# The last gV and the last gK of a decode-attention backward pass, each stored in two parts through two queues

## The chip, the cores and the metric

The kernel runs on one core of one Trainium2 chip. The metric is the device time of one execution in microseconds (us). Three runs of the kernel before took 887.74, 890.04 and 891.40 us; their median is 890.04 us. One more execution was taken with the profiler: it took 888.48 us, and its profile spans 886.3 us from the first to the last of the program's instructions.

## What is computed

One decoder block with pre-layernorm attention over a cache and a small ReLU network, for B = 2 sequences of one token, D = 640, H = 32 heads of width 128, a cache of Sk = 4096 positions, all in bf16. The output and the gradients of all inputs but one are wanted:

```python
def _A_ref(x, k_cache, v_cache, wq, wo):
    q = (x @ wq).reshape(B, Sq, Hq, Dh).transpose(0, 2, 1, 3)
    scores = einsum("bhqd,bhkd->bhqk", q, k_cache) * Dh ** -0.5
    p = softmax(scores)
    o = einsum("bhqk,bhkd->bhqd", p, v_cache)
    return o.transpose(0, 2, 1, 3).reshape(B, Sq, Hq * Dh) @ wo
h  = x + _A_ref(layernorm(x), k_cache, v_cache, wq, wo)
h2 = h + relu(layernorm(h) @ w1) @ w2
# outputs: h2, and the gradients to x, k_cache, v_cache, wq, wo, w1, w2 for a given grad_out
```

The two large results are the gradients to the caches: gK (`out_2`) and gV (`out_3`), each of 2 x 32 x 4096 x 128 bf16 numbers, which is 64 tiles of 1 MB (one for each pair of a sequence and a head). For one pair, gV is the outer product of the softmax weights with a row vector of 128, and gK the outer product of the scores' gradient with another such vector.

## The kernel before, in words

A tile of a cache or of its gradient is `[128 partitions, 32, 128]` bf16: partition p holds the 32 positions 32p to 32p+31, which are 8 KB that lie together in DRAM (`natural`, L440). So a store of one tile is 128 rows of 8 KB.

The work goes in two passes over the 64 pairs. The first (`p1_iter`, L452) loads K and V of a pair on SyncE's queue (L445), transposes K on TensorE, makes scores and softmax weights, and sums up what the later steps need of V. Between the passes, generators in the background (`middle_gen`, `fin_gen`, `gx_gen`) make the rest of the block and the gradients of the weights; `outer_tile` stores these from ScalarE's queue (L989). The second pass (`p2_iter`, L863) is at turn j, in this order:

- the last quarter of the scores' gradient of turn j-1 (`last_dp`, `score_grad`: the tile `gsp`, L858), and the rows `rb` for turn j (L882);
- two halves of gK of turn j-1 on VectorE (`outer_half`, L844), and its store from GpSimd's queue (L899);
- the V tile of turn j, loaded again as `Wt` or kept, transposed on TensorE in four groups (L424), copied out by ScalarE (L429), and multiplied with the gradient vector (L437);
- two halves of gV of turn j on VectorE (L844), in half of the pass with some rows on ScalarE (L930), and its store from GpSimd's queue (L931).

The first two turns store gV at L909, and the turns that run beside the first pass store gK at L941; neither concerns the last turn. The plan (L1160) ends with j = 63, whose gV is the last gV, and j = 64, which has only the last gK to make. A buffer goes back to its pool with `give`; the next writer of that buffer waits for the store's landing. After the last gK nothing takes a buffer, and the program ends when every queue's transfers have landed (SyncE waits for them at L1333).

GpSimd's queue carries only gV and gK stores in this part of the run, with a small copy (L884, `pp`) ahead of each turn. SyncE's queue carries loads, and two small stores of 10 rows of 256 B (`store_rows`, L675); the second of these is its last instruction before the end. At the start ScalarE's queue loads two inputs as 10 rows of 256 B (L208, L209).

Of the kernel before, what the change touches and what calls it, by code (L numbers as in the profile page):

```python
# [15 lines left out]
def kernel(  # L16
# [20 lines left out]
    nc = tc.nc  # L37
# [35 lines left out]
    def pst(shape, dtype, role, name):  # L73

        k = banks[role].pop(0)
        banks[role].append(k)
        return ps.tile(shape, dtype, tag=f"bank{k}", bufs=1, name=name)
# [11 lines left out]
    def take(tag, shape, name):  # L89
        assert free[tag] > 0, (tag, name)  # L90
        free[tag] -= 1
        k = homes[tag].pop(0)
        t = pools[k].tile(shape, BF16, tag=f"big{k}", bufs=1, name=name)
        home_of[id(t)] = (tag, k, t)
        return t

    def goes_to(tag):

        if owned[tag] > wanted.get(tag, len(pools)):
            for other in homes:  # L100
                if owned[other] < wanted.get(other, 0):
                    return other
        return tag

    def give(t, to=None):
        tag, k, _ = home_of.pop(id(t))
        to = to or goes_to(tag)
        owned[tag] -= 1
        owned[to] += 1
        free[to] += 1  # L110
        homes[to].append(k)
        given_at[k] = step[0]
# [282 lines left out]
    NP1 = len(pairs)  # L395
# [20 lines left out]
    def pair_transpose(nat, g, dve=False, busy=0):  # L416


        t_ps = pst([128, GT // 2, 128], FP32, "tps", "t_ps")
        warm(t_ps[:].rearrange("p j k -> p (j k)"), nat, g, busy)  # L420
        natf = nat[:].bitcast(FP32)
        for j in range(GT // 2):
            cc = (g * GT) // 2 + j
            nc.tensor.transpose(t_ps[:, j, :], natf[:, 2 * cc:2 * cc + 2, :].rearrange("p c k -> p (c k)"), ident_f[:])  # L424
        t_sb = mats.tile([128, GT // 2, 128], FP32, tag="XT", bufs=4, name="t_sb")
        if dve:
            nc.vector.tensor_copy(out=t_sb[:], in_=t_ps[:])  # L427
        else:
            nc.scalar.copy(out=t_sb[:], in_=t_ps[:])  # L429
        return t_sb  # L430

    def pair_matvec(dst, t_sb, g, vecs):
        v = t_sb[:].bitcast(BF16).rearrange("p j (k two) -> p j k two", two=2)
        for j in range(GT // 2):
            sc = g * GT + 2 * j
            for par in range(2):
                nc.tensor.matmul(dst[:, sc:sc + 2], lhsT=v[:, j, :, par], rhs=vecs[:, par, :],  # L437
                                 start=(par == 0), stop=(par == 1))

    def natural(cache, b, h):  # L440
        return cache[b, h].rearrange("(p sc) d -> p sc d", sc=NSC)
# [399 lines left out]
    def outer_half(dst, row, colp, k, short=0):  # L841
        n = HALF - short
        sl = slice(k * HALF, k * HALF + n)
        nc.vector.tensor_tensor(  # L844
            out=pairs_view(dst[:, sl, :]),
            in0=row.rearrange("p (a two) -> p a two", two=2)[:, None, :, :].to_broadcast([128, n, 64, 2]),
            in1=colp[:, sl, None, :].to_broadcast([128, n, 64, 2]), op=ALU.mult)

    def last_dp(j, c):

        b, h = turns[j]
        pair_matvec(c["dp"], c.pop("T3"), 3, gom[:, h, b, :, :])

    def score_grad(j, c):

        b, h = turns[j]
        gsp = small.tile([128, NSC, 2], BF16, tag="gsp", bufs=2, name="gsp")
        nc.vector.scalar_tensor_tensor(  # L858
            out=gsp[:], in0=c["dp"][:, :, None].to_broadcast([128, NSC, 2]), scalar=negdot[:, h, b:b + 1],
            in1=P_bf[:, b * H + h, :, None].to_broadcast([128, NSC, 2]), op0=ALU.add, op1=ALU.mult)  # L860
        return gsp

    def p2_iter(j, busy, act=0, own_gK=False, early=False):  # L863

        c = S2[j] if j < NP1 else None
        p = S2.get(j - 1)
        if p is not None:
            bp, hp = turns[j - 1]
            last_dp(j - 1, p)
            gsp = score_grad(j - 1, p)  # L870
        if c is not None:
            b, h = turns[j]
            go = gom[:, h, b, :, :]

            bank = pst([128, 512], FP32, "sps", "dp_ps")
            for k, col in enumerate((goc, qsc)):
                nc.tensor.matmul(bank[:, 128 + k * 128:256 + k * 128],  # L877
                                 lhsT=col[:, h, b:b + 1].to_broadcast([128, 128]), rhs=ident_bf[:],
                                 start=True, stop=True)
            c["dp"] = bank[:, 0:NSC]  # L880
            rb = mats.tile([128, 256], BF16, tag="rb", bufs=3, name="rb")
            nc.scalar.activation(out=rb[:], in_=bank[:, 128:384], func=ACT.Copy, scale=rt[:, b, h:h + 1])  # L882
            pp = small.tile([128, NSC, 2], BF16, tag="pp", bufs=2, name="pp")
            nc.gpsimd.tensor_copy(out=pp[:], in_=P_bf[:, b * H + h, :, None].to_broadcast([128, NSC, 2]))  # L884
            c.update(rb=rb, pp=pp)
            if act:
                pa = small.tile([128, 8], FP32, tag="pa", bufs=2, name="pa")
                nc.gpsimd.tensor_copy(out=pa[:], in_=P_bf[:, b * H + h, NSC - act:NSC])
            c["T0"] = pair_transpose(c["W"], 0, busy=busy)
        if p is not None:  # L890
            gK = take("g", [128, NSC, 128], "gK")
            outer_half(gK, p["rb"][:, 128:256], gsp, 0)
        yield
        if early:
            gV = take("g", [128, NSC, 128], "gV")
            outer_half(gV, c["rb"][:, 0:128], c["pp"], 0)
        if p is not None:
            outer_half(gK, p["rb"][:, 128:256], gsp, 1)
            nc.gpsimd.dma_start(out=natural(out_2, bp, hp), in_=gK[:])  # L899
            give(gK)  # L900
            del S2[j - 1]
        yield
        if c is None:
            return
        c["T1"] = pair_transpose(c["W"], 1, busy=busy)
        pair_matvec(c["dp"], c.pop("T0"), 0, go)
        if early:
            outer_half(gV, c["rb"][:, 0:128], c["pp"], 1)
            nc.gpsimd.dma_start(out=natural(out_3, b, h), in_=gV[:])  # L909
        yield  # L910
        c["T2"] = pair_transpose(c["W"], 2, busy=busy)
        pair_matvec(c["dp"], c.pop("T1"), 1, go)
        yield
        c["T3"] = pair_transpose(c["W"], 3, busy=busy)
        give(c["W"], "g" if j < H and j != 1 and owned["g"] < 3 else None)
        pair_matvec(c["dp"], c.pop("T2"), 2, go)
        if early:
            give(gV)
            yield
            last_dp(j, c)  # L920
            gsp = score_grad(j, c)
        else:
            gV = take("g", [128, NSC, 128], "gV")
            outer_half(gV, c["rb"][:, 0:128], c["pp"], 0)
            yield
            if own_gK:
                last_dp(j, c)
            outer_half(gV, c["rb"][:, 0:128], c["pp"], 1, act)
            for k in range(act):
                nc.scalar.activation(out=gV[:, NSC - act + k, :], in_=c["rb"][:, 0:128], func=ACT.Copy, scale=pa[:, k:k + 1])  # L930
            nc.gpsimd.dma_start(out=natural(out_3, b, h), in_=gV[:])  # L931
            give(gV)
            if own_gK:
                gsp = score_grad(j, c)
            yield
        if own_gK:
            gK = take("g", [128, NSC, 128], "gK")
            outer_half(gK, c["rb"][:, 128:256], gsp, 0)
            yield
            outer_half(gK, c["rb"][:, 128:256], gsp, 1)  # L940
            nc.gpsimd.dma_start(out=natural(out_2, b, h), in_=gK[:])  # L941
            give(gK)
            del S2[j]
            yield
# [275 lines left out]
    for n, (i, j) in enumerate(plan):  # L1220
# [18 lines left out]
        if j is not None:  # L1239
            while g2 is not None:  # L1240
                p2_step()
            if j < NP1:
                bg_until(("go", *turns[j]))
            g2 = p2_iter(j, 0, 8 if i is None and j <= H else 0, i is not None and plan[n + 1][1] is None, j < EARLY)
# [93 lines left out]
```

## Time and profile before

| | |
|---|---|
| median of 3 runs | 890.04 us (887.74 to 891.40) |
| profiled execution | 888.48 us |
| its span | 886.3 us |
| mean granted TensorE clock | 0.772 |
| busy: PE, DVE, ACT, POOL | 83%, 77%, 56%, 23% of the span |
| bytes moved | 361.85 MB, 408 GB/s over the span |
| last instruction of VectorE (second half of the last gK) ends | 869.40 us |
| last store issued (GpSimd, L899) | 869.70 us |
| span ends | 886.3 us |

The profile's page gives busy times of the engines, the span in 40 slices, the DMA queues with packets and bytes, and the issues with the time from issue to landing. Further views are taken from the trace: a timeline of instructions, waits (who waited for whom), and windows, which give for chosen stretches the busy time of each engine, the granted clock, the mean busy share of the core's 16 DMA engines ("DMA share": 0.06 is one engine of 16) and the rate in GB/s. The trace also keeps every DMA packet with its start, queue, duration and size, though not the number of the DMA engine that moved it. q0 is GpSimd's queue, q1 SyncE's, q10 ScalarE's.

### The profile page before, as it was taken

The page shows a single profiled execution, that of the slowest core. Times are in us where ns is not written, and L with a number is a line of the kernel's source. Part 1 is how long each engine was busy: PE and PEld are TensorE (multiplying, and loading weights), DVE is VectorE, ACT ScalarE, POOL GpSimd, SP SyncE. Part 2 cuts the span into 40 slices and gives each one's busy share as a digit, 9 for nine tenths or more (in the row PEclk, how much of TensorE's full clock was granted, in tenths as well). Part 3 has the DMA queues.
Part 4 walks back from the last instruction along what each step waited for, and adds up shares of the span by engine and source line. Part 5 has one row for each costly group of instructions (what it writes and reads, how often), then busy time and mean ns, then how long its engine had stood idle before and what let it go on. Part 6 is the DMA issues. An engine that isn't in the chain of part 4 may idle for free.

```text
span 886.3 us, 24732 instructions
## 1 busy us (share of the span) xinstructions
PE 738.8 (83%) x10143; PEld 618.2 (70%) x10143; DVE 681.3 (77%) x1281; ACT 498.8 (56%) x1292; POOL 204.1 (23%) x358
## 2 busy tenths in 40 slices
PE   4999899999999997988868767787877899867690
PEld 4887788888887886877757656665656667564550
DVE  2666787877788896876778887878788689989861
ACT  1444343446776664654536767777656766545570
POOL 1344433343312010000011332222222111111220
PEclk9999999999999999998995655555566755555555
DMA  9999999999879999999999999999999999999996
GB/s 380 423 420 414 417 409 417 425 423 412 332 295 402 423 423 426 422 426 425 414 398 396 418 421 421 420 413 420 419 416 403 417 425 420 425 425 425 425 424 275
DMA packets 56289, 361.85 MB, mean 408 GB/s; under 512 B 5680, under 2 KB 11760, under 8 KB 15472
## 3 DMA queue, kind: packets, MB, share of 16 engines
q1 hardware_dynamic: 34520, 211.13, 57.8%
q0 software_dynamic: 18432, 134.23, 36.5%
q10 hardware_dynamic: 3224, 14.92, 4.1%
q8 instruction: 80, 1.31, 0.5%
q14 instruction: 33, 0.27, 0.1%
HBM read 211.11 MB, written 149.13 MB: 406 GB/s over the span
## 4 chain that ended last, share of the span: by engine, by line
PE 35%; DMA 34%; DVE 16%; ACT 7%; issue 5%; SPq 0%; POOL 0%; ACTq 0%; POOLq 0%; DVEq 0%
DMA Vt<-in_A_v_cache_dram 15%; PE t_ps L424 14%; DMA out_dram<-gK 11%; PE m_ps L460 9%; DVE gK L844 4%; DVE gV L844 4%; DMA out_dram<-gV 3%; ACT gV L930 3%; PE s_ps L437 3%; DMA wqs<-in_A_wq_dram 3%; DVE pk L470 2%; PE u_ps L498 2%; ACT t_sb L429 2%; PE dp_ps L437 2%; DVE gxj L678 2%
## 5 line engine op out<-in xcount | busy, mean ns | idle before, releaser
L429 ACT COPY t_sb<-t_ps 128x512 f32<-128x512 f32 x479 | 273.1, 587 | 192.4 <-PE t_ps L424 188.6
L437 PEld LDWEIGHTS <-t_sb 128*128 128x128 bf16 x4096 | 178.9, 102 | 63.8 <-ACT t_sb L429 36.2
L424 PE MATMUL t_ps<-ident_f,Wt 128*128 128x128 f32 x832 | 198.6, 389 | 0.9 <-ACT t_sb L429 0.9
L470 DVE TENSOR_TENSOR pk<-Kt,ep 128x2048 bf16<-128x2048 bf16 (+1 forms) x128 | 152.6, 1193 | 47.1 <-ACT ep L524 29.0
L460 PE MATMUL m_ps<-pk,Vt 128*128 128x129 bf16 x2048 | 172.0, 223 | 19.9 <-DMA Vt<-in_A_v_cache_dram 18.8
L844 DVE TENSOR_TENSOR gK<-rb,gsp 128x2048 bf16<-128x2048 bf16 x128 | 153.4, 1227 | 13.3 <-DMA out_dram<-gV 8.5
L460 PEld LDWEIGHTS <-Vt 128*128 128x128 bf16 x2048 | 125.6, 99 | 50.2 <-issue 28.4
L424 PEld LDWEIGHTS t_ps<-ident_f,Wt 128*128 128x128 f32 x832 | 138.2, 202 | 31.9 <-issue 25.2
L424 PE MATMUL t_ps<-ident_f,Kt 128*128 128x128 f32 x1024 | 156.0, 286 | 2.5 <-DMA Kt<-in_A_k_cache_dram 1.9
L844 DVE TENSOR_TENSOR gV<-rb,pp 128x2048 bf16<-128x2048 bf16 (+1 forms) x128 | 142.7, 1139 | 16.3 <-DMA out_dram<-gK 9.9
L486 POOL COPY pk<-ep 128x16 bf16<-128x16 bf16 x80 | 83.6, 1046 | 158.4 <-ACT ep L524 80.0
L424 PEld LDWEIGHTS t_ps<-ident_f,Kt 128*128 128x128 f32 x1024 | 113.9, 145 | 5.0 <-ACT t_sb L429 2.7
L437 PE MATMUL dp_ps<-gom,t_sb 128*128 128x2 bf16 x2048 | 96.0, 168 | 25.1 <-ACT t_sb L429 24.7
L931 POOL DMA_DIRECT2D out_dram<-gV x62 | 33.0, 533 | 305.3 <-DVE gsp L858 135.1
L437 PE MATMUL s_ps<-qm,t_sb 128*128 128x2 bf16 x2048 | 87.4, 164 | 1.5 <-DVE t_sb L427 1.5
L986 ACT CAST ot<-o_ps 128x512 bf16<-128x512 f32 (+3 forms) x152 | 67.5, 491 | 8.4 <-DMA out_dram<-ot 5.2
L588 ACT CAST MT<-m_ps 128x128 bf16<-128x128 f32 x64 | 17.0, 266 | 94.5 <-PE m_ps L460 94.4
L899 POOL DMA_DIRECT2D out_dram<-gK x53 | 28.2, 533 | 135.4 <-DVE gK L844 104.9
L882 ACT ACTIVATE rb<-dp_ps,rt 128x256 bf16<-128x256 f32 x64 | 30.2, 472 | 44.7 <-PE dp_ps L877 43.4
L678 DVE CUSTOM_DVE_ANT_0 hbc<-wo_t,hbc 128x640 bf16<-128x640 bf16 x64 | 52.8, 825 | 0.3
L678 DVE CUSTOM_DVE_ANT_0 gxj<-wqs,gqr 128x1024 bf16<-128x1024 bf16 x40 | 48.7, 1217 | 1.0 <-DMA wqs<-in_A_wq_dram 0.8
L930 ACT ACTIVATE gV<-rb,pa 128x128 bf16<-128x128 bf16 x152 | 46.5, 392 | 3.9 <-DMA out_dram<-gK 3.9
(205 smaller groups left out, 758.2 us busy)
## 6 DMA issues: line engine op xcount, KB each, us to landing
Kt<-in_A_k_cache_dram SPq DMA_DIRECT2D x64, 1024.0 KB, 19.4
Vt<-in_A_v_cache_dram SPq DMA_DIRECT2D x64, 1024.0 KB, 15.5
out_dram<-gV POOLq DMA_DIRECT2D x64, 1024.0 KB, 14.9
out_dram<-gK POOLq DMA_DIRECT2D x64, 1024.0 KB, 15.0
Wt<-in_A_v_cache_dram SPq DMA_DIRECT2D x52, 1024.0 KB, 11.6
wq_t<-in_A_wq_dram SPq DMA_DIRECT2D x5, 1024.0 KB, 7.8
wo_t<-in_A_wo_dram SPq DMA_DIRECT2D x4, 1280.0 KB, 17.6
wqs<-in_A_wq_dram SPq DMA_DIRECT2D x5, 1024.0 KB, 22.3
```

The lines of the kernel that those rows point to most:

```text
L424: nc.tensor.transpose(t_ps[:, j, :], natf[:, 2 * cc:2 * cc + 2, :].rearrange("p c k -> p (c k)"), ident_f[:])
L429: nc.scalar.copy(out=t_sb[:], in_=t_ps[:])
L437: nc.tensor.matmul(dst[:, sc:sc + 2], lhsT=v[:, j, :, par], rhs=vecs[:, par, :], start=(par == 0), stop=(par == 1))
L460: nc.tensor.matmul(r["m"][:, 0:129], lhsT=r["V"][:, sc, :], rhs=r["pk"][sc // HALF][:, sc % HALF, 0:129], start=(sc == 0), stop=(sc == NSC ...
L470: nc.vector.tensor_tensor(out=p["pk"][k][:, 0:n, 0:128].rearrange("p s (a two) -> p s a two", two=2), in0=p["K"][:, sl, :].rearrange("p s ...
L486: nc.gpsimd.tensor_copy(out=col, in_=e)
L678: nc.vector.tensor_tensor_reduce(out=junk[0:kc, 0:width], in0=in0, in1=in1, scale=1.0, scalar=0.0, op0=ALU.mult, op1=ALU.add, accum_out=acc)
L844: nc.vector.tensor_tensor(out=pairs_view(dst[:, sl, :]), in0=row.rearrange("p (a two) -> p a two", two=2)[:, None, :, :].to_broadcast([128 ...
L882: nc.scalar.activation(out=rb[:], in_=bank[:, 128:384], func=ACT.Copy, scale=rt[:, b, h:h + 1])
L930: nc.scalar.activation(out=gV[:, NSC - act + k, :], in_=c["rb"][:, 0:128], func=ACT.Copy, scale=pa[:, k:k + 1])
L931: nc.gpsimd.dma_start(out=natural(out_3, b, h), in_=gV[:])
L986: nc.scalar.copy(out=ot[0:P, k, n0:n0 + nn], in_=o_ps[0:P, 0:nn])
```

## The change

The store of gK at L899 and the store of gV at L931 become calls of a helper. For all turns but the last it issues what was issued before. For the last gV (j = 63) and the last gK (j = 64) it issues partitions 0 to 119 from GpSimd's queue and partitions 120 to 127 from SyncE's queue.

```diff
+    def store(out_ap, t, last):
+
+        n = 120 if last else 128
+        nc.gpsimd.dma_start(out=out_ap[0:n], in_=t[0:n])
+        if last:
+            nc.sync.dma_start(out=out_ap[n:128], in_=t[n:128])
+        give(t)
@@ p2_iter
-            nc.gpsimd.dma_start(out=natural(out_2, bp, hp), in_=gK[:])
-            give(gK)
+            store(natural(out_2, bp, hp), gK, c is None)
@@ p2_iter
-            nc.gpsimd.dma_start(out=natural(out_3, b, h), in_=gV[:])
-            give(gV)
+            store(natural(out_3, b, h), gV, j == NP1 - 1)
```

The order of the instructions on TensorE, VectorE, ScalarE and GpSimd is the same in both kernels. SyncE has two more: after its last 10-row store, the 8 rows of the last gV and the 8 rows of the last gK.

## The prediction

> **What bounds the kernel now.** I read the slices first. The line "DMA" stands at 9 in nearly every slice, so transfers set the pace; only the last slice falls off, and the change touches nothing ahead of it.
>
> ```profile
> DMA  9999999999879999999999999999999999999996
> ...
> DMA packets 56289, 361.85 MB, mean 408 GB/s; under 512 B 5680, under 2 KB 11760, under 8 KB 15472
> ...
> q0 software_dynamic: 18432, 134.23, 36.5%
> ```
>
> Then the timeline of GpSimd's last issues. VectorE ends at 869.40; the last store is out 0.3 us later, and yet the span lasts to 886.3. So 16 us belong to transfers alone.
>
> ```profile
> 862.68 0.53 POOL L899 DMA_DIRECT2D out_dram<-gK  x1 [5.25 <-DVE gK L844]
> 864.96 0.53 POOL L931 DMA_DIRECT2D out_dram<-gV  x1 [1.74 <-DVE gV L844]
> 869.70 0.53 POOL L899 DMA_DIRECT2D out_dram<-gK  x1 [4.21 <-DVE gK L844]
> ```
>
> Then windows over those 16 us. The last two columns are the share of 16 DMA engines and the rate.
>
> ```profile
> 870.00:876.00 6.00, 0.00 (x0) 0.00 (x0) 0.00 (x0) 0.00 (x0) 0.23 (x1) 0.50 1.01 425
> 876.00:878.00 2.00, 0.00 (x0) 0.00 (x0) 0.00 (x0) 0.00 (x0) 0.00 (x0) 0.50 0.78 330
> 878.00:879.40 1.40, 0.00 (x0) 0.00 (x0) 0.00 (x0) 0.00 (x0) 0.00 (x0) 0.50 0.34 140
> 879.40:881.20 1.80, 0.00 (x0) 0.00 (x0) 0.00 (x0) 0.00 (x0) 0.00 (x0) 0.50 0.18 77
> 881.20:881.70 0.50, 0.00 (x0) 0.00 (x0) 0.00 (x0) 0.00 (x0) 0.00 (x0) 0.50 0.12 49
> 881.70:884.10 2.40, 0.00 (x0) 0.00 (x0) 0.00 (x0) 0.00 (x0) 0.00 (x0) 0.50 0.06 24
> 884.10:886.30 2.20, 0.00 (x0) 0.00 (x0) 0.00 (x0) 0.00 (x0) 0.00 (x0) 0.50 0.00 0
> ```
>
> The shares 0.18, 0.12 and 0.06 are three, two and one engine of 16: three still write after 879.4, two after 881.2, one from 881.7 to 884.1. That last stretch is 8 packets of 8 KB, one started every 0.306 us (2.45 us): one engine's sixteenth of a 128-row store. The waits of SyncE's queue say whose rows they are:
>
> ```profile
> SPq L1333 <- DMA out_dram<-gV: 42.6, 1, 42.6
> ...
> SPq L1333 <- DMA out_dram<-gK: 2.4, 1, 2.4
> ```
>
> The last gV has landed at 882.1 and the last gK 2.4 us later, so the late engine (I call it A) writes its 8 gV rows and then its 8 gK rows. By the packet list it ends at 884.13; the next ends at 881.68 (B), the others at 881.18, 879.45, and then 878.9 and earlier. **What is at stake is the tail of A**, not the 1 MB.
>
> **Which engine is A?** The packets carry no engine number, but an engine's packets follow each other with a fixed overlap of 3 ns, so its chain can be followed. Nearly all 8 KB packets in the last 40 us take 309 ns; those of 311 to 367 ns form one chain, which ends as A. So A is not merely last, it is slow: up to 876 its packets keep taking longer. In the second 10-row store of SyncE's queue one of the ten 256 B packets lies inside that chain (start from the span's start, queue, ns, bytes):
>
> ```
> 842.510 q0 312 8192
> 842.818 q1 18 256
> 842.832 q0 320 8192
> ```
>
> In the first one, at 781.6, one of the ten again runs straight into a lengthened packet. How many engines a small transfer uses follows from the page: 5680 packets under 512 B. The 350 other transfers (128 on q0, 203 on q1, 19 on q10) leave 16 completion packets of 4 B each, 5600; the 80 left are four 10-row transfers with 10 rows and 10 completions each. Ten rows use ten engines, and A was one of them both times.
>
> **The change, part by part.**
>
> 1. *GpSimd stores 120 rows.* Two issues of 0.53 us stay two issues. No row shows a 120-row store; an issue could lie between 0.50 us (120/128 of the row) and twice the row, 1.07 us. I take 0.53, its nearest row. It is covered either way: A's gK rows start at 881.7, 12 us after the issue, and the earliest engine's at about 873.3, 3 us after it. Without that cover it would cost at most 0.5 us.
> 2. *How the 120 rows fall on engines.* This is the open cost. Best for the change: fifteen engines take 8 rows each and A takes none; A then loses 16 packets and would end at 884.13 - 16 x 0.306 = 879.2, and B sets the end. Middle: A keeps its 8. Worst of the near cases: eight engines take 15 rows each, 14 more in the two stores, +4.3 us. The nearest rows are the 10-row ones, where the number of engines was a divisor of the rows: 120 = 15 x 8. Both 10-row transfers used A; if a transfer on fewer engines uses a fixed first set, fifteen include those ten, and A keeps its rows. I take 0, keeping -4.9 and +4.3 us on A.
> 3. *SyncE stores 8 rows, twice.* The issue row is 0.32 us (L675), on a queue idle from 839.5 on; nothing but the end stands behind it, so its new wait for VectorE holds up nobody. The 10-row store issued at 839.16 had its first packet at 842.7 and its last completion at 843.8. Issued near 865 and 870, the new rows should start near 868.5 and 873.3, take turns with the other queues' packets, and be gone by 875. They add one 8 KB packet to each of eight engines, twice. If A is among the eight (8 in 10, when the eight are part of the ten), A ends 2 x 0.306 = 0.61 us later; if not, nothing moves. I take +0.61, bounds 0 and +0.61.
> 4. *Two more completions at the end.* They land 8 us before A does; the end waits for A. Nothing.
>
> [...]
>
> **Sum.** 888.48 + 0 + 0.61 = 889.1 us for the profiled execution. The median of the runs is 1.56 us above that execution, so I forecast 890.04 + 0.61 = **890.6 us**. A measurement of this kernel can tell about 0.5% (4.45 us) from no change; this is within it.
>
> **Rivals.**
>
> *A is relieved.* The engine left out is A, in both stores (A would end at 879.2) or in the first alone (881.7). The end goes to B at 881.68, or 882.29 with the two SyncE rows on it: 884.13 less that is 1.84 to 2.45 us, so 887.6 to 888.2 us. For it: A is the slow engine and last; leaving out any fixed engine aims at something like it. Against it: A took part in both 10-row transfers. It can't give more than that, since B and the third are late too.
>
> *The 120 rows crowd onto fewer engines* (the slower side). If the store goes to eight engines, those have 15 rows instead of 8, 14 more over both stores: with A among them and the two SyncE rows, 4.28 + 0.61 = 4.9 us, 894.9 us, slower by 0.55%. It decides from the point where A itself has 9 rows or more in a store: each costs 0.306 us. If one engine took all 120, 37 us a store. Against it: ten rows used ten engines, not eight; for it: no store of an odd share of 128 on GpSimd's queue is in the trace.
>
> *The change does nothing that lasts.* The order of the other engines' instructions is the same, SyncE's two stores come after all else there, and if A is in neither set the end stays at 890.0 us. I count it with the forecast.
>
> **How the numbers follow.** Forecast (A keeps its rows, 0 to +0.61 us): 0.60. Relief: 0.25. Crowding: 0.10. Something not thought of: 0.05. The three runs before spread 3.7 us, so a median may move by half of that, 1.85 us. Range: from the relief's middle, 887.9, less about 1.1, to 890.6 plus 1.85: 886.8 to 892.5 us; it leaves out the crowding and the rest. Relief is -0.2% to -0.3%, so faster by over 0.5% needs scatter on top: 0.05. Slower by over 0.5% is most of the crowding: 0.09. Within: 0.86.
>
> **What would show it.** Windows over the tail: if A keeps its rows, the last stretch at 0.06 stays about 2.5 us long and ends some 0.6 us later after the last issue; the gap between the landings of gV and gK on SyncE stays 2.4 us. If A is relieved, that stretch shrinks below 0.6 us and the end comes within 12.6 us of the last issue instead of 14.4. If the rows crowd, a stretch near 0.50 (eight engines of 16) several us long appears. The packets on q0 tell the engines: a 120-row store's 8 KB packets number 240 in all, and the packets on q1 should be 16 rows and 16 completions more. The forecast is wrong if the slow engine isn't fixed from run to run, or if the odd shape makes GpSimd's issue much longer than 1 us.

## The result, and the profile after

The changed kernel takes 893.26 us (median of 13 runs, 891.81 to 897.09), the kernel before 888.81 us in the same rounds (13 runs, 887.53 to 891.68). The ratio of the runs is 1.0055, 95% interval 1.004 to 1.007: slower by 4.9 us (3.6 to 6.2), where the two medians differ by 4.45. In what follows, differences and their intervals are worked out from such ratios. The forecast was 890.6 us, and its range ended at 892.5. The profiled execution took 892.54 us, 4.06 more than that of before, with a span of 890.2 us.

The page of the changed kernel; its DMA line still stands at 8 or 9 up to the last slice, and the packets are those that the change must give:

```profile
span 890.2 us, 24736 instructions
...
DMA  9999999999889999999999999999999999999995
...
DMA packets 56321, 361.85 MB, mean 406 GB/s; under 512 B 5712, under 2 KB 11792, under 8 KB 15504
...
q1 hardware_dynamic: 34552, 211.26, 57.7%
q0 software_dynamic: 18432, 134.09, 36.4%
```

SyncE's queue q1 has 32 packets more (34,520 before): 16 rows and 16 completions. GpSimd's q0 has as many as before, though it lost 16 rows: so each 120-row store left 24 completions of 4 B instead of 16. That fits fifteen engines with 8 rows and one completion each, and a sixteenth without rows that posts 9 (8 and one); in the packet list, a run of ten 4 B packets of q0, 6 ns apart and without an 8 KB packet between them, stands at 871.92 to 871.97 us.

GpSimd's last issues in the timeline of the changed kernel (start, duration, line, what it stores, idle time before):

```profile
861.36 0.53 POOL L866 DMA_DIRECT2D out_dram<-gK  x1 [5.24 <-DVE gK L844]
863.63 0.54 POOL L866 DMA_DIRECT2D out_dram<-gV  x1 [1.74 <-DVE gV L844]
868.37 0.53 POOL L866 DMA_DIRECT2D out_dram<-gK  x1 [4.21 <-DVE gK L844]
```

and SyncE's:

```profile
839.56 0.32 SPq L675 DMA_DIRECT2D out_dram<-orow  x1
863.36 0.31 SPq L868 DMA_DIRECT2D out_dram<-gV  x1
868.11 0.28 SPq L868 DMA_DIRECT2D out_dram<-gK  x1
```

The last issue comes 1.33 us *earlier* than before (868.37 against 869.70), and the last row lands later: at 888.19, 19.8 us after that issue, where before it was 884.13, 14.4 us after. So in these two executions all of the loss lies in the transfers of the tail. Windows over it, after (the last two columns are the share of 16 DMA engines and GB/s):

```profile
868.00:872.00 4.00, 0.00 (x0) 0.00 (x0) 0.08 (x1) 0.00 (x0) 0.53 (x1) 0.50 1.01 411
872.00:876.00 4.00, 0.00 (x0) 0.00 (x0) 0.00 (x0) 0.00 (x0) 0.00 (x0) 0.50 0.97 352
876.00:880.00 4.00, 0.00 (x0) 0.00 (x0) 0.00 (x0) 0.00 (x0) 0.00 (x0) 0.50 0.78 282
880.00:884.00 4.00, 0.00 (x0) 0.00 (x0) 0.00 (x0) 0.00 (x0) 0.00 (x0) 0.50 0.25 90
884.00:888.20 4.20, 0.00 (x0) 0.00 (x0) 0.00 (x0) 0.00 (x0) 0.00 (x0) 0.50 0.06 25
```

and before, where one stretch of the same bounds stands beside the second of these:

```profile
872.00:876.00 4.00, 0.00 (x0) 0.00 (x0) 0.00 (x0) 0.00 (x0) 0.00 (x0) 0.50 1.02 426
```

Read the last two columns together. From 872 to 876 the engines are busy nearly all the time in both kernels, but move 352 GB/s instead of 426: 0.97/1.02 of the busy share, 0.83 of the bytes. **With packets of the same size, a full share with a lower rate means that each packet takes longer.** The last stretch, in which one engine writes alone (0.06), lasts 4.1 us (884.08 to 888.19) instead of 2.4.

The packet list says it row by row. Before, the last 256 packets of 8 KB on q0 take 309 ns each. After, the last 240 on q0 take 357 ns in the mean (some of them still belong to earlier stores), and the 16 rows of q1 up to 1329. In the 17 us up to the last landing, 53 of 343 packets of 8 KB on q0 are over 320 ns, and the list holds 15.0 us of engine time above 309 ns a packet, against 0.09 us before. The engine that ends last has this chain from 876.85 on, in ns (the list has no engine numbers, but an engine's packets follow each other, and a completion packet stands behind its share of each store):

```
931 640 593 533 329 309 526 607 609 659 644 | 8 x 309 (gV) | 8 x 309 (gK), ends 888.19
```

The 11 packets ahead of its own 16 rows belong to earlier, unsplit stores. They take 6.38 us where 11 x 309 ns would be 3.40: 2.98 us of the 4.06 by which the transfers end later. Followed further back, the chain most likely leads (at 871.92 two chains meet in the list) to one with a row of each of SyncE's stores, at 866.98 and 871.45, 309 ns each, and before that to lengthened packets of 314 to 369 ns (861.18 to 865.74), as the slow engine A has them. So the last engine is probably A again, and these two rows are another 0.61 us. SyncE's waits at the end show the last 8 rows once more:

```profile
SPq L1339 <- DMA out_dram<-gV: 17.7, 1, 17.7
...
SPq L1339 <- DMA out_dram<-gK: 2.4, 1, 2.4
```

gK lands 2.4 us after gV, as before: the last engine has 8 rows of gK, at the usual speed. It is late because it was held up *earlier*, while other engines moved rows of the split stores.

### The profile page after: what moved, and what is told of

Same layout as the page of the kernel before. It is cut to its first block, busy times and chain, and to the rows that moved or that the text cites. A ratio compares the mean times of both kernels' runs of the same rounds, so it can differ in the third digit from the quotient of the medians.

```text
span 890.2 us, 24736 instructions
## 1 busy us (share of the span) xinstructions
PE 740.7 (83%) x10143; PEld 620.8 (70%) x10143; DVE 681.2 (77%) x1281; ACT 498.9 (56%) x1292; POOL 203.4 (23%) x358
## 4 chain that ended last, share of the span: by engine, by line
PE 38%; DMA 29%; DVE 17%; ACT 7%; issue 5%; POOL 0%; ACTq 0%; SPq 0%; POOLq 0%; DVEq 0%
PE t_ps L424 16%; DMA Vt<-in_A_v_cache_dram 13%; DMA out_dram<-gK 9%; PE m_ps L460 9%; DVE gK L844 5%; DVE gV L844 4%; DMA out_dram<-gV 3%; PE s_ps L437 3%; ACT gV L937 3%; PE u_ps L498 3%; DVE pk L470 2%; DMA wqs<-in_A_wq_dram 2%; ACT t_sb L429 2%; DVE gxj L678 2%; PE dp_ps L437 2%
## 5 line engine op out<-in xcount | busy, mean ns | idle before, releaser
L460 PEld LDWEIGHTS <-Vt 128*128 128x128 bf16 x2048 | 125.8, 99 | 49.8 <-issue 29.0
```

The lines of the kernel that those rows point to most:

```text
L460: nc.tensor.matmul(r["m"][:, 0:129], lhsT=r["V"][:, sc, :], rhs=r["pk"][sc // HALF][:, sc % HALF, 0:129], start=(sc == 0), stop=(sc == NSC ...
```

## The experiments

Two theories. **First:** the number of rows of a store decides how its rows fall on the engines. With 128 rows, by this theory, the engines don't meet; with 120 they get in each other's way, and packets grow long. **Second:** SyncE's 8 rows do it, by a second queue that cuts into the engines' chains. In all edits `store` is the helper of the change, and the lines are shown against the changed kernel (the last edit against the kernel before); `...` stands for lines left out. Medians stand beside those of the kernel before on the same chip.

### One part alone: the 120 rows, or the 8

Only the 120 rows, with 8 rows of the last gV and gK not stored:

```diff
         nc.gpsimd.dma_start(out=out_ap[0:n], in_=t[0:n])
-        if last:
-            nc.sync.dma_start(out=out_ap[n:128], in_=t[n:128])
```

> Only the 120 rows are stored from GpSimd's queue; the 8 rows of the last gV and the last gK are left out of the output. Theory 1 (the 120-row store itself does the harm: its rows fall on the engines in another way than those of a 128-row store, so that engines get into each other's way): the packets on q0 are lengthened after 871 us as in the changed kernel (mean near 357 ns over the last two stores), and the time stays 3 to 5 us above before. Theory 2 (SyncE's 8-row stores do it: eight engines read eight neighbouring partitions at once): packets at 309 ns, time within 1 us of before.

Measured: 892.38 us (12 runs) against 889.17, ratio 1.0041 (1.0022 to 1.0061), +3.7 us. In the 17 us up to the last landing its 8 KB packets on q0 take 349 ns in the mean, 12.3 us of engine time above 309. Most of the loss is there without any row from SyncE.

The other part: 128 rows from GpSimd, and SyncE copies the last 8 partitions to a scratch tensor.

```diff
-        nc.gpsimd.dma_start(out=out_ap[0:n], in_=t[0:n])
...
+        nc.gpsimd.dma_start(out=out_ap, in_=t[:])
         if last:
-            nc.sync.dma_start(out=out_ap[n:128], in_=t[n:128])
+            sc = nc.dram_tensor(f"aside{len(asides)}", [8, NSC, 128], BF16).ap()
...
+            nc.sync.dma_start(out=sc, in_=t[120:128])
```

> GpSimd stores all 128 rows as before; SyncE also stores partitions 120 to 127 of the last gV and the last gK, to a place of their own in DRAM that is no output. Theory 1: 0 to 0.6 us above before (two more packets on some engines), only the 16 packets on q1 are long. Theory 2: 3 to 5 us above before, with long packets on q0 too.

Measured: 890.62 us (12) against 889.17, ratio 1.0014 (0.9994 to 1.0033), +1.2 us. GpSimd's packets take 316 ns, 2.95 us of engine time too much; SyncE's own rows still take up to 1732 ns. So the 8 rows run into others too, but there are few of them; at most 2.9 us by the interval, and not told from nothing.

### Is it the engine left without rows?

With a cut at 112 the same two queues are used, but the number of rows divides by the 16 engines: 16 x 7 rows.

```diff
-        n = 120 if last else 128
+        n = 112 if last else 128
```

> The cut at partition 112 in place of 120, so that both parts are multiples of 16 and every engine can have the same number of rows. If what harms is that one engine is left without rows: time as before, within 1 us. Theory 1 in the form that any store of other than 128 rows is dealt to the engines in neighbouring rows (7 each): long packets on q0, 2 to 5 us above before. Theory 2: 16 neighbouring partitions read at once, 3 us or more above before, longest packets on q1.

Measured: 892.01 us (12) against 889.17, ratio 1.0024 (1.0003 to 1.0045), +2.1 us. Each 112-row store leaves 16 completions, as a 128-row one does, so no engine sits out; yet the packets of q0 take 388 ns in the last 17 us, 21.6 us of engine time too much, more than in the changed kernel. So long packets need neither an idle engine nor its extra completions. (SyncE's 16 rows are in this run too; their packets take 3.7 us too much.) The time is less bad than the packets; probably less of the delay fell on the last engine, but that wasn't followed.

### The first theory made large

All 115 stores that go through the helper take 120 rows; 8 rows of each are not stored. SyncE stores nothing of them.

```diff
-        n = 120 if last else 128
+        n = 120
         nc.gpsimd.dma_start(out=out_ap[0:n], in_=t[0:n])
-        if last:
-            nc.sync.dma_start(out=out_ap[n:128], in_=t[n:128])
```

> All 115 stores of the helper (not only the last two) take 120 rows, and 8 rows of each are left out of the output: 7.5 MB less to move, 18 us at 424 GB/s. Theory 1: the last two stores of the changed kernel lost about 15 us of engine time on q0, 7.5 us each, 0.47 us of 16 engines; 115 of them cost 54 us, so 36 us above before (between 15 and 60, since loads in between may hide or add to it), with a mean of q0's 8 KB packets near 357 ns. Theory 2 and the theory that the tail alone matters: 10 to 18 us below before, packets near 310 ns.

Measured: 943.49 us (4) against 889.17, ratio 1.0598 (1.0558 to 1.0638): **54 us more, for 7.5 MB less to move.** Its windows in the second pass:

```profile
750.00:800.00 50.00, 35.45 (x295) 26.47 (x296) 38.97 (x58) 23.98 (x56) 6.77 (x14) 0.53 0.98 371
800.00:850.00 50.00, 28.41 (x242) 21.86 (x242) 38.29 (x52) 20.91 (x49) 5.83 (x12) 0.53 0.97 359
```

and of the kernel before:

```profile
750.00:800.00 50.00, 39.15 (x339) 29.05 (x338) 46.07 (x67) 27.67 (x64) 7.36 (x15) 0.53 1.01 425
800.00:850.00 50.00, 37.34 (x286) 24.87 (x285) 42.29 (x61) 28.30 (x58) 10.37 (x20) 0.53 1.01 424
```

It is the picture of the tail, held for hundreds of us: share nearly full, rate down by 13% and 15%. The page counts 6600 packets under 512 B, 5680 + 115 x 8: eight more completions a store, as reckoned above. All packets together took 877.9 us per engine before (mean of 16) and 909.6 here, 31.7 more. As the 920 rows left out would have taken 18.1 off, packets grew by 49.8 us per engine. The span is 56.9 us longer (943.2 against 886.3): 31.7 of it are packets, and for the other 25 an engine had, in the mean, no packet; what it waited for then was not followed. 8 KB packets of q0 went from 315 to 352 ns in the mean.

### Which side: the partitions or the place in DRAM

Twins: every one of the 115 stores stays whole, and GpSimd copies 8 more rows of the tile to scratch. They differ in the partitions alone that the 8 rows are read from: neighbours 0 to 7, or 0, 4, 8 to 28.

```diff
+        nc.gpsimd.dma_start(out=out_ap, in_=t[:])
...
+        nc.gpsimd.dma_start(out=sc, in_=t[0:8])
```

```diff
+        nc.gpsimd.dma_start(out=out_ap, in_=t[:])
...
+        nc.gpsimd.dma_start(out=sc, in_=t[0:32:4])
```

> Each of the helper's 115 stores keeps its 128 rows on GpSimd's queue and is followed there by 8 rows more, partitions 0 to 7, to a place of their own in DRAM: 7.5 MB more, 18 us at 424 GB/s. If engines that read neighbouring partitions at the same time hold each other up (theory 1 in the form of a shared way out of the partitions): the 8 packets take near 1 us each, as the longest ones on q1 did in the changed kernel, 5.6 us of engine time a store, so 30 to 70 us above before, and clearly more than its twin. If the cause lies on the DRAM side or in the number of rows: the same time as its twin.

> The twin: the same 8 rows more after each of the 115 stores, to the same place, but read from partitions 0, 4, 8 to 28 in place of 0 to 7. Theory of the shared way out: 12 to 25 us above before (the bytes alone) and few long packets. Theory of the DRAM side or of the number of rows: the same as its twin.

Measured: neighbours 1005.21 us (4 runs), ratio 1.1292 (1.1257 to 1.1326), +116 us; apart 934.32 us (4), 1.0493 (1.0466 to 1.0521), +45 us; before 889.28. Rows, bytes and target are the same. Packet time per engine rises by 65.6 us with neighbours and 30.9 apart, of which the 920 rows themselves are 18.1 (at 315 ns): 47.5 against 12.8 us of lengthening. On GpSimd's queue 808 packets of 8 KB take over 500 ns with neighbours, 184 apart and 239 before; their means are 336, 314 and 315 ns. A window of each, neighbours first:

```profile
750.00:800.00 50.00, 34.11 (x281) 24.18 (x280) 22.26 (x25) 22.28 (x49) 10.05 (x21) 0.54 0.95 372
```

```profile
750.00:800.00 50.00, 35.77 (x311) 27.28 (x310) 43.62 (x64) 23.93 (x55) 14.14 (x27) 0.50 0.97 384
```

**In these copies the choice of partitions that are read decides** (47.5 us of lengthening per engine against 12.8), so here packets are held up on the side of the tile, not of DRAM. That is shown; what reads of neighbouring partitions wait for is not, nor which row of a 120-row store goes to which engine. That the 120-row stores lose their time in the same way fits it but is argued.

Both cost more than expected (30 to 70 us and 12 to 25 us). The packets cover 65.6 us of the 116 and 30.9 of the 45; the rest was not followed. One candidate is to be seen in GpSimd's waits of the kernel with rows apart (in total us, times, longest):

```profile
POOL out_dram L867 <- DMA out_dram<-gV: 99.9, 26, 6.9
POOL out_dram L867 <- DMA out_dram<-gK: 52.6, 19, 5.7
```

With two issues a tile, GpSimd is held at issues until earlier stores of its own have landed; the kernel before has no such wait, and the one with 120 rows throughout has a single one of 1.4 us. How much of the 45 us this is stays open: the kernel with 120 rows throughout has its 25 us without packets in spite of that single wait.

### Halves: 64 rows, or half of each row

By rows:

```diff
-        n = 120 if last else 128
-        nc.gpsimd.dma_start(out=out_ap[0:n], in_=t[0:n])
-        if last:
-            nc.sync.dma_start(out=out_ap[n:128], in_=t[n:128])
+        for n in (0, 64):
+            nc.gpsimd.dma_start(out=out_ap[n:n + 64], in_=t[n:n + 64])
```

By columns:

```diff
-        n = 120 if last else 128
-        nc.gpsimd.dma_start(out=out_ap[0:n], in_=t[0:n])
-        if last:
-            nc.sync.dma_start(out=out_ap[n:128], in_=t[n:128])
+        for n in (0, 16):
+            nc.gpsimd.dma_start(out=out_ap[:, n:n + 16, :], in_=t[:, n:n + 16, :])
```

> Each of the helper's 115 stores leaves in two parts of 64 rows from GpSimd's queue, partitions 0 to 63 and 64 to 127. Each engine then has 4 rows of each part and all 16 are used evenly. Theory 1 (rows of a store with other than 128 rows are dealt so that engines read the same few groups of partitions): 30 to 80 us above before, q0's 8 KB packets well above 315 ns on the mean. If only uneven numbers of rows do harm: within 5 us of before.

> The control to the halves by rows: each of the 115 stores leaves in two parts of 128 rows with half of each row (4 KB). As many transfers and bytes in each, but rows from all partitions. Theory 1: within 8 us of before, no packets lengthened. If twice as many stores on GpSimd's queue do harm by themselves: the same excess as with the halves by rows.

Measured: by rows 950.77 us (4), ratio 1.0692 (1.0662 to 1.0723), +62 us; by columns 899.73 us (4), 1.0131 (1.0107 to 1.0154), +11 us; before 888.86. Both have 230 issues of 512 KB, and all partitions are stored. A window of each, first by rows:

```profile
750.00:800.00 50.00, 27.39 (x250) 20.73 (x247) 34.55 (x46) 19.20 (x44) 11.81 (x24) 0.50 0.98 358
```

then by columns:

```profile
750.00:800.00 50.00, 40.19 (x308) 28.45 (x308) 49.69 (x71) 26.71 (x63) 13.88 (x27) 0.52 1.02 419
```

With 64 rows an issue the rate falls to 358 GB/s at 0.98, and 8 KB packets of q0 take 361 ns; with 128 rows of half the length it stays at 419, and a 4 KB packet takes 161 ns (159 when undisturbed). So it isn't the second issue or the smaller store that lengthens packets, but that a store reads half of the partitions; and 64 rows, a multiple of 16, do it as well as 120. The 11 us by columns were more than expected: packet time rises by 13.0 us per engine (with 14,720 more packets of rows), which covers them. GpSimd's waits at its issues are there too:

```profile
POOL out_dram L866 <- DMA out_dram<-gV: 51.5, 29, 4.3
POOL out_dram L866 <- DMA out_dram<-gK: 49.4, 26, 5.0
```

What they cost was not told apart. Taking the 11 us off leaves some 50 of the 62 us to the halving by rows.

### One of the two stores

Only the last gV split:

```diff
-            store(natural(out_2, bp, hp), gK, c is None)
+            store(natural(out_2, bp, hp), gK, False)
```

Only the last gK:

```diff
-            store(natural(out_3, b, h), gV, j == NP1 - 1)
+            store(natural(out_3, b, h), gV, False)
```

> Only the last gV leaves in two parts; the last gK leaves whole, as before. Theory 1: each split store costs about half of the change's 4 to 5 us, so 1.5 to 3 us above before, with long packets on q0 from about 871 us that stop before the end. If only what stands at the very end counts: nothing measurable, below 1 us.

> Only the last gK leaves in two parts; the last gV leaves whole, as before. The gV alone came out at 0.7 us above before (-0.8 to +2.1). If the two parts of the change add up, the gK alone carries the rest: 3 to 4.5 us above before. If it takes both 120-row stores at work beside each other: 0 to 1.5 us above before.

Measured: gV alone 889.80 us (12) against 889.28, ratio 1.0008 (0.9991 to 1.0024); gK alone 890.42 us (12) against 888.86, 1.0021 (1.0002 to 1.0041). In each, q0's packets are held up by about 10 us of engine time in the 17 us up to the last landing (9.9 and 11.0), yet the end moves by 0.7 and 1.9 us. So the delay in all and the delay of the *last* engine are different things. Both splits together cost 4.9 us (3.6 to 6.2), more than the sum of the two, 2.6; the intervals are too wide to call that more than an impression. The gV alone lies below the 1.5 to 3 us that the first theory named, the gK alone between its two expectations.

### The queues exchanged

120 rows from SyncE, 8 from GpSimd:

```diff
-        nc.gpsimd.dma_start(out=out_ap[0:n], in_=t[0:n])
+        (nc.sync if last else nc.gpsimd).dma_start(out=out_ap[0:n], in_=t[0:n])
         if last:
-            nc.sync.dma_start(out=out_ap[n:128], in_=t[n:128])
+            nc.gpsimd.dma_start(out=out_ap[n:128], in_=t[n:128])
```

> The 120 rows of the last gV and gK leave from SyncE's queue and the 8 rows from GpSimd's. If the dealing of rows is a matter of the number of rows and not of the queue: 3 to 5 us above before, long packets on q1. If it is GpSimd's queue alone that deals 120 rows badly: within 1.5 us of before.

Measured: 891.86 us (9) against 888.86, ratio 1.0027 (1.0015 to 1.004), +2.4 us, between the two expectations. The packets decide: 8 KB packets that start after 870 us take 394 ns in the mean on SyncE's queue and 408 on GpSimd's. It is no matter of GpSimd's queue. The page also gives the engines once more:

```profile
q1 hardware_dynamic: 34790, 213.09, 58.3%
```

270 packets more than before: 240 rows and 30 completions, so 15 engines for each 120-row store, with no completions from the sixteenth on this queue.

### Is the last engine slow because of GpSimd's queue?

The last six turns' stores, whole, from SyncE:

```diff
+        (nc.sync if last else nc.gpsimd).dma_start(out=out_ap, in_=t[:])
...
-            nc.gpsimd.dma_start(out=natural(out_2, bp, hp), in_=gK[:])
...
+            store(natural(out_2, bp, hp), gK, j > NP1 - 6)
...
-            nc.gpsimd.dma_start(out=natural(out_3, b, h), in_=gV[:])
...
+            store(natural(out_3, b, h), gV, j >= NP1 - 6)
```

> The gV and gK of the last six turns leave whole, 128 rows, from SyncE's queue in place of GpSimd's. If the late engine is slow because of GpSimd's queue: its packets become regular (309 ns) in the last 40 us and the tail in which one engine writes alone shortens from 2.4 us towards nothing, 1 to 4 us below before. If it is slow by itself: time as before within 1 us, the tail as long as before. By theory 1 no long packets either way, as all rows leave in stores of 128.

Measured: 888.50 us (12) against 889.28, ratio 0.9985 (0.997 to 1.0), -1.3 us: the best of all, though not told from the kernel before. Whole stores from SyncE have hardly any long packets: 311 ns in the mean over the last 17 us, where those of the 120-row stores from SyncE took 394. Its tail:

```profile
880.00:882.00 2.00, 0.00 (x0) 0.00 (x0) 0.00 (x0) 0.00 (x0) 0.00 (x0) 0.50 0.43 180
882.00:884.00 2.00, 0.00 (x0) 0.00 (x0) 0.00 (x0) 0.00 (x0) 0.00 (x0) 0.50 0.16 66
```

A few engines still end late (0.16 is two to three of 16), but the last one writes alone for 0.7 us (883.71 to 884.41) instead of 2.4, and the last row lands 11.0 us after the last issue instead of 14.4. That is what was named for a slowness that comes from GpSimd's queue; the gain in time was not as clear. One chain of packets takes 313 to 361 ns up to 859.7 us, but GpSimd's own last packet stands at 860.6; after that, lengthened packets spread over several chains. So whether the engine is slow because of GpSimd's queue stays open.

## Why the prediction was wrong

**What bounds the kernel: right.** The tail of transfers sets the end, and the last engine's chain in it; the loss lies there. One reading was wrong: the packets of A do not keep taking longer up to 876. In the list of before, the last 8 KB packets over 309 ns stand at 866.40 (327 ns) and 869.43 (400 ns).

**Part 1, GpSimd's issue: right.** 0.53 and 0.54 us, as taken, and covered.

**Part 2, "How the 120 rows fall on engines": the step that failed.** Its count was right: fifteen engines take 8 rows each, and A keeps its 8 (the gap between the landings stayed 2.4 us; an engine ran out of rows early, but it was not the one that ends last). Its price was wrong. Each row was set at 0.306 us whatever store it belongs to, and the bounds of -4.9 and +4.3 us varied only *how many* rows an engine takes. The runs show that how *long* a row takes depends on the store's number of rows: 309 ns for each of the last 256 packets before, 357 in the mean for the last 240 after, and 352 instead of 315 over the run when all stores have 120. And the delay isn't kept to those rows: on the engine that ends last, 11 packets of earlier, unsplit stores took 2.98 us more. So the term in the sum that stood as 0 was about +4 us, with the two splits alone (no row from SyncE) measured at +3.7 (2.0 to 5.4).

**Part 3, SyncE's 8 rows: the timing right, the size small as said.** They were issued at 863.36 and 868.11, started some 3.5 us later, and were gone by 874.6; but they took 0.3 to 1.3 us each, not 0.3. Eight rows copied aside twice moved the time by 1.2 us (-0.5 to 2.9), which agrees with the 0 to 0.61 us of the forecast and with more. By its most likely chain, A had one row of each store, at 309 ns: the 0.61 us that was taken.

**Part 4, completions: right.** SyncE's last one stands at 875.1, 13 us before the last row lands.

**The rivals.** Relief didn't come, since the engine without rows was another. The crowding rival named 894.9 us, and the measured difference is its 4.9 us; but no engine had more rows, and no stretch at 0.50 of several us appeared. That its size fits is chance: it was worked out from 14 more rows of the 120-row stores on A, and A had none more. Its own argument against, that ten rows used ten engines, pointed the right way: fifteen took part.

**What the forecast could have asked.** The gV and gK stores in the trace of before all have 128 rows, and the 10-row ones move 256 B a row in 18 ns, so no row there shows what a split store costs. The step should have kept the duration of a row open, not its engine alone: in the same trace, 866 of 16,384 8 KB packets on q0 took over 320 ns, up to 1.72 us, so that a row doesn't always take 309 ns was to be seen.

## What to carry to other kernels

When DMA bounds a stage, read the busy share and the rate side by side: a share that stays full while GB/s falls means, with packets of the same size, that each takes longer. Then fewer bytes may not help: here 7.5 MB less went with 54 us more. In a kernel like this one, keep stores of a full tile on all 128 partitions in one issue; if one must be divided, divide the row, not the partitions (+11 us against +62 us over 115 tiles here). And at the end of a program ask what delays the last engine, whosever packets these are: 10 to 30 us of added engine time in the tail, by the edit, moved the end by 0.7 to 4.9 us, and not in that order.

## What the runs showed of the hardware that was not expected

- Stores of 120, 112 or 64 partitions go with longer packets, the 120-row ones from GpSimd's queue as from SyncE's: 8 KB packets went from 309 ns undisturbed to means of 349 to 394, single ones to over 1 us.
- Eight rows more per tile cost 45 us when read from every fourth partition and 116 us when read from neighbours.
- A 120-row store on GpSimd's queue leaves 24 completion packets, on SyncE's 15.
- With two issues a tile, GpSimd waited at its issues for its earlier transfers (100.9 us in all with halves by columns, 152.5 with the 8 rows apart, 174.8 with halves by rows). With one issue a tile there is no such wait in the kernel before, and a single one of 1.4 us in the changed kernel and in the one with 120 rows throughout.
